# One-token attention plus feed-forward: output in 20 rows of 32, two hardware repeats on TensorE, and the last V in two loads

## The chip, the cores and the metric

The kernel runs on one NeuronCore of one Trainium2 chip. The metric is the device time of one execution in microseconds (us). Every number below comes from result lists, from the profile of one execution of a kernel, or from the packet and instruction records in its trace. The span in a profile is about 2 us shorter than the device time of the same execution (1285.6 against 1287.6 us for the kernel before). In the views, PE is TensorE, PEld its loading of weights, DVE is VectorE, ACT is ScalarE, and SPq and DVEq are instructions that SyncE and VectorE handle without computing (the issue of a load, a wait). A hardware repeat is a loop whose body stands in the program once (in the trace of the changed kernel each turn of the new repeats leaves a counter step of 0.032 to 0.042 us and a branch on TensorE, 0.207 to 0.231 us where it was taken); PV is the product of the softmax weights with V.

## The reference

A decode step: one token `x` of 640 numbers is layer-normalised, then goes through attention over a cache of 32 heads with 32,768 positions, and beside it through a small gated feed-forward part; both results are added to `x`.

```python
x = A_x                                    # (1, 1, 640) bf16
xn = _layernorm(x)
q = (xn @ wq).reshape(B, Sq, 32, 128)      # 32 heads of 128
scores = einsum("bhqd,bhkd->bhqk", q, k_cache) * 128 ** -0.5
o = einsum("bhqk,bhkd->bhqd", softmax(scores), v_cache)
return x + o.reshape(...) @ wo + (silu(xn @ w_gate) * (xn @ w_up)) @ w_down
# k_cache, v_cache: (1, 32, 32768, 128) bf16: 8 MiB per head and cache
```

Each cache byte is used once. 64 loads of 8 MiB make 537 of the 554 MB that the kernel reads.

## The kernel before

SyncE issues all large loads, in one order, into a ring of three slots. A slot is loaded again when its user is done: K when the scores of its head are made, V when its PV product is made.

```python
TAIL = [128, 64, 32, 32]                  # the last V in four loads
WTAIL = [8, 8, 8, 5, 2, 1]                # the output weights in six
...
elif u[0] == "k":
    e.dma_start(ring[:, s, :], kv_src(A_k_cache, u[1], 0, NJ)).then_inc(s_slot[s], 16)
    owner[s] = (s_qk, NHF * (u[1] + 1))   # this slot is free after these scores
elif u == LASTV:
    for i, n in enumerate(TAIL): ...      # one load and one semaphore for each piece
elif u[0] == "v":
    e.dma_start(ring[:, s, :], kv_src(A_v_cache, u[1], 0, NJ)).then_inc(s_slot[s], 16)
    owner[s] = (s_pv, u[1] + 1)           # free after this PV
```

TensorE's program is written out for q and for the first two heads, then a hardware loop runs ten times over three heads, and then the tail is written out. The parts that the change touches:

```python
for b in range(NQB):                      # q: 8 x 5 matmuls of 512 columns
    for c in range(NCD):
        mm = t.matmul(bank[b], lhsT=xnb[:, c, :], rhs=wq_v[:, c, b * 512:(b + 1) * 512], ...)
...
for j in range(first, first + PARTS[part], W):       # PV of one head: 64 matmuls of 512 columns
    mm = t.matmul(O, lhsT=P[:, h % PR, j:j + W], rhs=ring[:, s, j * DH:(j + W) * DH], ...)
...
# the end: acc (128 x 5) holds feed-forward and attention, summed in PSUM
v.tensor_tensor(out=outb[:, :], in0=xr[:, :], in1=acc, op=ALU.add)           # + x, VectorE
t.matmul(orow_ps, lhsT=outb[:, :], rhs=ident[:, :], start=True, stop=True)    # turn to 5 rows of 128
v.tensor_copy(out=orow[:, :], in_=orow_ps)                                    # to bf16 in SBUF
e.dma_start(out[0, 0:1, :].rearrange("o (c m) -> (o c) m", c=NCD), orow[:, :])
```

Of the kernel before, what the change touches and what calls it, by code (L numbers as in the profile page):

```python
# [5 lines left out]
ALU = mybir.AluOpType  # L6
ACTF = mybir.ActivationFunctionType
AX = mybir.AxisListType
BF16 = mybir.dt.bfloat16
F32 = mybir.dt.float32  # L10


def bass_parallel_sum__gqa_block_cached__swiglu_ffn__decode_kernel(
# [13 lines left out]
    H = A_k_cache.shape[1]  # L27
    SK = A_k_cache.shape[2]
    DH = A_k_cache.shape[3]
    F = B_w_gate.shape[1]  # L30
    assert DH == 128 and A_wq.shape[1] == H * DH and D % 128 == 0 and SK % 128 == 0
    NCD = D // 128
    NJ = SK // 128
# [4 lines left out]
    CE = NJ * DH  # L38
# [3 lines left out]
    NQB = (H * DH) // 512  # L42
    SLOTS = 3
    H0, PER = 2, 3
    PR = 3
    SR = 3
    TAIL = [128, 64, 32, 32]
    RB = DH // 32
    OC = H * DH // 128
    WTAIL = [8, 8, 8, 5, 2, 1]  # L50
    PARTS = [64, 64, 128]
# [27 lines left out]
    with ExitStack() as es:  # L79
        def sbt(name, shape, dtype):  # L80
            return es.enter_context(nc.sbuf_tensor(name, shape, dtype))
# [16 lines left out]
        ot = sbt("ot", [128, OC], BF16)  # L98
        hcol = sbt("hcol", [128, FB + 1], BF16)
        par = sbt("par", [128, 2], F32)  # L100
        sg = sbt("sg", [128, 2, FB], F32)
        one1 = sbt("one1", [1, 1], BF16)
        xf = sbt("xf", [128, NCD], F32)
        xr = sbt("xr", [128, NCD], F32)
        orow = sbt("orow", [NCD, 128], BF16)
        xc = sbt("xc", [128, NCD], F32)
        xq = sbt("xq", [128, NCD], F32)
        xn = sbt("xn", [128, NCD], BF16)
        outb = sbt("outb", [128, NCD], BF16)
        st = sbt("st", [128, 8], F32)  # L110
        pmax = sbt("pmax", [128, SR], F32)
        m1 = sbt("m1", [1, SR], F32)
# [91 lines left out]
            return tile[:, bass.ds(start, n)]  # L204

        with nc.psum_tensor("ps8", [128, 8, 512], F32) as ps8:
            bank = [ps8[:, b, :] for b in range(8)]
            O = ps8[0:W, 4, :]
            OL = ps8[:, 5, 0:1]
# [1 line left out]
            acc = ps8[:, 6, 0:NCD]  # L211
            fold_ps = ps8[:, 6, 8:9]
            misc = ps8[:, 7, :]
            orow_ps = ps8[0:NCD, 5, 128:256]
            ffn = bank[0]

            @block.sync
            def sp(e):
                owner = {}
                for u in units:  # L220
                    s = slot_of[u]
                    if s in owner:
                        e.wait_ge(*owner.pop(s))
                    if u[0] == "wq":
                        owner[s] = (s_q, NQB)
                    elif u[0] == "k":
                        e.dma_start(ring[:, s, :], kv_src(A_k_cache, u[1], 0, NJ)).then_inc(s_slot[s], 16)
                        owner[s] = (s_qk, NHF * (u[1] + 1))
                    elif u == LASTV:
                        j = 0  # L230
                        for i, n in enumerate(TAIL):
                            e.dma_start(ring[:, s, j * DH:(j + n) * DH],
                                        kv_src(A_v_cache, u[1], j, n)).then_inc(s_tail[i], 16)
                            j += n
                    elif u[0] == "v":
                        e.dma_start(ring[:, s, :], kv_src(A_v_cache, u[1], 0, NJ)).then_inc(s_slot[s], 16)
                        owner[s] = (s_pv, u[1] + 1)
                    elif u[0] == "ffn":
                        e.dma_start(wg, B_w_gate.rearrange("(p c) n -> p (c n)", c=NCD)).then_inc(s_ffn[0], 16)
                        e.dma_start(wu, B_w_up.rearrange("(p c) n -> p (c n)", c=NCD)).then_inc(s_ffn[1], 16)  # L240
                        e.dma_start(flat[:, d0:d0 + FM * D], B_w_down[0:FM * 128, :].rearrange(
                            "(p j) n -> p (j n)", j=FM)).then_inc(s_ffn[2], 16)
                        e.dma_start(wdr, B_w_down[FM * 128:F, :].rearrange(
                            "f (t n) -> (f t) n", t=2)).then_inc(s_ffn[2], 16)
                    else:
                        wo_src = A_wo.rearrange("(p j) n -> p (j n)", j=OC)
                        j = 0
                        for i, n in enumerate(WTAIL):
                            e.dma_start(wo[:, j * D:(j + n) * D], wo_src[:, j * D:(j + n) * D]).then_inc(s_wo[i], 16)  # L249
                            j += n  # L250
                e.wait_ge(s_fin, 2)
                e.dma_start(out[0, 0:1, :].rearrange("o (c m) -> (o c) m", c=NCD), orow[:, :]).then_inc(s_out, 16)

            @block.gpsimd
            def pool(g):
                n = [0]

                def done(ins):
                    ins.then_inc(s_const, 1)
                    n[0] += 1  # L260
                    g.wait_ge(s_const, n[0])

                for t in (ident, identf):
                    done(g.memset(t[:, :], 0.0))
                    done(g.affine_select(out=t[:, :], in_=t[:, :], compare_op=ALU.not_equal, fill=1.0, base=0,
                                         pattern=[[-1, 128]], channel_multiplier=1))
                done(g.memset(blk[:, :], 0.0))
                for a in range(RB):
                    done(g.tensor_copy(out=fold32[a * 32:(a + 1) * 32, :],
                                       in_=ident[a * 32:(a + 1) * 32, a * 32:a * 32 + OC]))  # L270
                for a in range(RB):
                    done(g.memset(blk[a * 32:(a + 1) * 32, a:a + 1], 1.0))
                assert n[0] == 5 + 2 * RB
                g.wait_ge(s_out, 16)

            @block.tensor
            def pe(t):
# [14 lines left out]

                t.wait_ge(s_a, 11)
                t.wait_ge(s_wq, 16)
                for b in range(NQB):
                    for c in range(NCD):
                        mm = t.matmul(bank[b], lhsT=xnb[:, c, :], rhs=wq_v[:, c, b * 512:(b + 1) * 512],  # L297
                                      start=(c == 0), stop=(c == NCD - 1))
                    mm.then_inc(s_q, 1)
                t.wait_ge(s_qc, NQB)  # L300
                t.wait_ge(s_const, 4)

                def again(out, lhsT, rhs, stop):

# [9 lines left out]
                def scores(h):  # L314
                    kv = ring[:, slot_of[("k", h)], :].rearrange("p (j d) -> p j d", d=DH)
                    for i in range(NHF):
# [9 lines left out]
                                mm = again(ob, ident[:, :], src, g == DH // G - 1)  # L326
                        mm.then_inc(s_qk, 1)

                def pv_part(h, part):
                    s = slot_of[("v", h)]  # L330
                    if part == 0:
                        wait(s_exp, h, lambda h: h + 1)
                        wait(s_o4, h, lambda h: h)
                        wait(s_slot[s], h, lambda h: 16 * use_of[("v", h)])
                    first = sum(PARTS[:part])
                    for j in range(first, first + PARTS[part], W):
                        mm = t.matmul(O, lhsT=P[:, h % PR, j:j + W], rhs=ring[:, s, j * DH:(j + W) * DH],  # L337
                                      start=(j == 0), stop=(j + W == NJ))
                    if part == len(PARTS) - 1:
                        mm.then_inc(s_pv, 1)  # L340
# [66 lines left out]
                def down():  # L407
                    t.wait_ge(s_ffn[2], 32)
                    t.wait_ge(s_fd, 6)
                    for j in range(FM):  # L410
                        for c in range(NCD):
                            t.matmul(acc[:, c:c + 1], lhsT=wd_v[:, j, c, :], rhs=hcol[:, j:j + 1],
                                     start=(j == 0 and c == 0), stop=False, skip_group_check=True)
                    for half in range(2):
                        a, b = half * (D // 2), (half + 1) * (D // 2)
                        for c in range(a // 128, (b + 127) // 128):
                            m0, m1 = max(a, c * 128), min(b, c * 128 + 128)
                            t.matmul(acc[m0 - c * 128:m1 - c * 128, c:c + 1], lhsT=wdr[:, m0 - a:m1 - a],
                                     rhs=hcol[:, FM + half:FM + half + 1],
                                     start=False, stop=False, skip_group_check=True)  # L420
# [21 lines left out]
                fold(H - 2)  # L442
                pv_last(range(1, len(TAIL))).then_inc(s_pv, 1)
                hidden_part(0)
                t.wait_ge(s_const, 5 + 2 * RB)
                t.wait_ge(s_ob, 1)
                t.matmul(op, lhsT=oblk[:, :, :], rhs=fold32[:, :], start=True, stop=True).then_inc(s_op, 1)
                hidden_part(1).then_inc(s_f, 1)
# [1 line left out]
                t.wait_ge(s_ot, 1)  # L450
                project().then_inc(s_att, 1)
                t.wait_ge(s_fin, 1)
                t.matmul(orow_ps, lhsT=outb[:, :], rhs=ident[:, :], start=True, stop=True).then_inc(s_or, 1)

            @block.scalar
            def act(a):
# [50 lines left out]
            def dve(v):  # L507
# [78 lines left out]
                def twice(i):  # L586
# [8 lines left out]
                v.wait_ge(s_rz, H)  # L595
                v.tensor_scalar(out=ocol[:, h:h + 1], in0=OL, scalar1=rzb[:, h % SR:h % SR + 1],
                                scalar2=None, op0=ALU.mult).then_inc(s_ov, 1)
                v.wait_ge(s_const, 5 + 2 * RB)
                v.wait_ge(s_ov, H + 1)
                v.tensor_tensor(out=oblk[:, :, :], in0=ocol[:, :, None].to_broadcast([128, H, RB]),  # L600
                                in1=blk[:, None, :].to_broadcast([128, H, RB]), op=ALU.mult).then_inc(s_ob, 1)
# [12 lines left out]
                                op=ALU.mult).then_inc(s_fd, 1)  # L614
                v.tensor_scalar(out=hcol[:, FM:FM + 2], in0=par[:, :], scalar1=sg[:, 0, FM:FB],
                                scalar2=ffn[:, FB + FM:2 * FB], op0=ALU.mult, op1=ALU.mult).then_inc(s_fd, 1)
                v.wait_ge(s_xr, 1)
                v.wait_ge(s_att, 1)
                v.tensor_tensor(out=outb[:, :], in0=xr[:, :], in1=acc, op=ALU.add).then_inc(s_fin, 1)
                v.wait_ge(s_or, 1)  # L620
                v.tensor_copy(out=orow[:, :], in_=orow_ps).then_inc(s_fin, 1)

# [29 lines left out]
```

## Time and profile before

| | value | from |
|---|---|---|
| device time | 1287.33 us (1287.29 to 1287.57, 3 runs) | result |
| loads on queue q1 | 554.00 MB, 99.7% of sixteen DMA engines' span | page, part 3 |
| TensorE, VectorE busy | 81%, 52% | page, part 1 |
| one 8 MiB load after the other | every 19.35 us, first to last head | packet records |

The page of the kernel before, cut to its span, the busy time of TensorE, the DMA rows of the 40 slices (tenths busy, then GB/s) and the DMA queues (packets, MB, share of 16 engines):

```profile
span 1285.6 us, 9851 instructions
...
PE 1042.0 (81%) x5154; PEld 260.9 (20%) x3235; DVE 672.2 (52%) x409; ACT 52.1 (4%) x139; POOL 2.5 (0%) x17
...
DMA  9999999999999999999999999999999999999998
...
q1 hardware_dynamic: 11242, 554.00, 99.7%
q8 instruction: 9, 0.15, 0.0%
```

The DMA row has no slice under 9 until the last. The kernel's length is the time that the sixteen engines need for these bytes, plus 1.03 us before the first packet and 3.07 us after the last weights have landed (packet records). A chain of waits that names K, PE and DVE by turns through the middle of such a kernel is true and of no use: it shows what released each issue, and every issue was early. The timeline of the kernel before shows how early (start, length, engine, line, operation, count):

```profile
15.35 10.43 PE L297 MATMUL ps<-ring 128*128 128x512 bf16 x39 [10.75 <-DMA ring<-in_A_wq_dram]
...
79.41 0.33 SPq L236 DMA_DIRECT2D ring<-in_A_v_cache_dram  x1
...
86.95 7.07 PE L337 MATMUL ps<-ring,P 128*4 128x512 bf16 x32
...
94.05 0.33 SPq L227 DMA_DIRECT2D ring<-in_A_k_cache_dram  x1
```

The issue at 94.05 us loads K3, after the first head's PV. The load before it (V1, issued at 79.41 us) keeps the engines busy until about 112 us (its last completion write is at 112.02 us). The last stretch is another matter. The chain of waits of the kernel before, its last pieces (start, length, what):

```profile
1253.03 28.77 DMA ring<-in_A_wo_dram
...
1281.85 1.49 PE ps L428 x40
...
1283.36 0.02 DVEq L618
...
1283.43 0.17 DVE outb L619
...
1283.65 0.28 PE ps L453
...
1283.95 0.28 DVE orow L621
```

After the fourth piece of the output weights has landed there is nothing to hide behind: projection, a separate wait instruction of VectorE (L618), add of x, turn (a matmul that transposes), cast, then the issue of the output, in the timeline:

```profile
1284.26 0.36 SPq L252 DMA_DIRECT2D out_dram<-orow  x1
```

### The profile page before, as it was taken

Reading aid. Unit: us, or ns where it says so; the run is one execution under the profiler, and the core shown is the slowest. Engines: PE = TensorE matmul, PEld = TensorE weight load, DVE = VectorE, ACT = ScalarE, POOL = GpSimd, SP = SyncE. Lnnn points to the kernel's source line nnn. Section 1 sums busy time; section 2 is a strip of 40 time slices with the busy share of each in tenths; the row PEclk is TensorE's granted clock in tenths of the full one; section 3 lists DMA queues with packets and bytes.
Section 4 is the critical chain, followed back from the end, with each engine's and each line's share of the span. In section 5 each row is a group of like instructions: output and inputs, shape, how many; then the busy total and the mean of one; then the engine's idle time right before and its main releaser. Section 6 shows DMA issues by size and latency. Waiting matters only on the chain.

```text
span 1285.6 us, 9851 instructions
## 1 busy us (share of the span) xinstructions
PE 1042.0 (81%) x5154; PEld 260.9 (20%) x3235; DVE 672.2 (52%) x409; ACT 52.1 (4%) x139; POOL 2.5 (0%) x17
## 2 busy tenths in 40 slices
PE   3599777889787799778788777898777798778797
PEld 1012112221112221112221112221112221112227
DVE  0855665445665446664446664446664446654441
ACT  2000000000000000000000000000000000000000
POOL 0000000000000000000000000000000000000000
PEclk9799888999888898888998888998888998888995
DMA  9999999999999999999999999999999999999998
GB/s 424 425 445 433 427 430 441 428 432 440 432 432 428 440 430 430 442 430 432 428 440 430 430 442 430 432 428 440 430 430 442 430 432 428 440 430 430 442 413 365
DMA packets 11256, 554.17 MB, mean 431 GB/s; under 512 B 1259, under 2 KB 1516, under 8 KB 1772
## 3 DMA queue, kind: packets, MB, share of 16 engines
q1 hardware_dynamic: 11242, 554.00, 99.7%
q8 instruction: 9, 0.15, 0.0%
q14 instruction: 3, 0.02, 0.0%
q10 hardware_dynamic: 2, 0.00, 0.0%
HBM read 553.99 MB, written 0.00 MB: 431 GB/s over the span
## 4 chain that ended last, share of the span: by engine, by line
DMA 53%; PE 28%; DVE 12%; issue 6%; SPq 0%; DVEq 0%
DMA ring<-in_A_k_cache_dram 51%; PE ps L337 17%; DVE ring L554 12%; PE ps L305 9%; DMA ring<-in_A_wo_dram 2%; PE ps L324 1%; PE ps L379 0%; PE ps L373 0%; PE ps L367 0%; PE ps L428 0%; SPq L249 0%; DVEq L554 0%; DVE sc L560 0%; DVE pmax L566 0%; DVE m L569 0%
## 5 line engine op out<-in xcount | busy, mean ns | idle before, releaser
L554 DVE TENSOR_TENSOR ring<-ring,qb 128x8192 bf16<-128x8192 bf16 x128 | 557.8, 4420 | 315.6 <-DMA ring<-in_A_k_cache_dram 315.6
L305 PE MATMUL ps<-ring,ident 128*128 128x512 bf16 x1920 | 498.4, 418 | 0.0
L337 PE MATMUL ps<-ring,P 128*4 128x512 bf16 x1984 | 443.3, 379 | 0.0
L324 PE MATMUL ps<-ring,ident 128*128 128x512 bf16 x128 | 56.1, 439 | 220.1 <-DVE ring L554 219.7
L337 PEld LDWEIGHTS ps<-ring,P 128*4 128x4 bf16 x1984 | 163.4, 85 | 237.8
L324 PEld LDWEIGHTS ps<-ring,ident 128*128 128x128 bf16 x128 | 12.6, 99 | 618.3 <-DVE ring L554 359.5
L560 DVE TENSOR_REDUCE sc<-ps 128x64 f32<-128x512 f32 x128 | 82.2, 683 | 63.4 <-PE ps L305 63.4
L572 DVE TENSOR_SCALAR negb<-ps 128x1 f32<-128x1 f32 x32 | 5.1, 159 | 108.4 <-PE ps L379 108.4
L480 ACT ACTIVATE P<-sc,negb 128x256 bf16<-128x256 f32 x32 | 16.2, 507 | 957.7 <-DVE negb L572 957.7
L569 DVE TENSOR_REDUCE m<-ps 1x1 f32<-1x128 f32 x32 | 8.9, 279 | 85.2 <-PE ps L373 85.2
L359 PEld LDWEIGHTS ps<-identf,o 4*128 4x128 f32 x248 | 30.7, 190 | 13.1 <-issue 13.1
L359 PE MATMUL ps<-identf,o 4*128 4x1 f32 x248 | 33.3, 251 | 0.0
L367 PEld LDWEIGHTS ps<-rsum,ones 128*128 128x128 f32 x64 | 12.1, 190 | 99.7 <-issue 98.9
L471 ACT ACTIVATE o<-ps,rzb 4x512 f32<-4x512 f32 x31 | 21.0, 678 | 6.2 <-PE ps L337 6.2
L297 PE MATMUL ps<-ring 128*128 128x512 bf16 x39 | 10.4, 428 | 10.8 <-DMA ring<-in_A_wq_dram 10.7
L476 ACT ACTIVATE ocol<-ps 128x1 f32 (+1 forms) x31 | 5.4, 173 | 222.4 <-PE ps L359 222.4
L566 DVE TENSOR_REDUCE pmax<-sc 128x1 f32<-128x256 f32 x32 | 13.4, 420 | 0.0
L373 PE MATMUL ps<-identf,pmax 128*1 128x128 f32 x64 | 12.2, 273 | 1.2 <-DVE pmax L566 1.2
L379 PE MATMUL ps<-m,ones 1*128 1x1 f32 x64 | 12.1, 256 | 0.4 <-DVE m L569 0.4
L379 PEld LDWEIGHTS ps<-m,ones 1*128 1x128 f32 x64 | 9.4, 182 | 14.2 <-issue 13.5
L403 PE MATMUL ps<-xn,ring 128*128 128x1 bf16 x140 | 8.3, 196 | 1.3 <-issue 1.3
L542 DVE RECIPROCAL rzb<-ps 128x1 f32<-128x1 f32 x32 | 5.0, 157 | 8.1 <-PE ps L367 8.1
(66 smaller groups left out, 82.5 us busy)
## 6 DMA issues: line engine op xcount, KB each, us to landing
ring<-in_A_wq_dram SPq DMA_DIRECT2D x1, 5120.0 KB, 15.2
ring<-in_A_v_cache_dram SPq DMA_DIRECT2D x1, 4096.0 KB, 31.8
ring<-in_A_wo_dram SPq DMA_DIRECT2D x3, 1280.0 KB, 24.7
ring<-in_B_w_gate_dram SPq DMA_DIRECT2D x1, 2160.0 KB, 23.2
ring<-in_B_w_up_dram SPq DMA_DIRECT2D x1, 2160.0 KB, 27.9
ring<-in_B_w_down_dram SPq DMA_DIRECT2D x1, 2080.0 KB, 31.3
ring<-in_A_v_cache_dram SPq DMA_DIRECT2D x1, 2048.0 KB, 36.4
ring<-in_A_v_cache_dram SPq DMA_DIRECT2D x2, 1024.0 KB, 39.4
```

Source lines behind the costliest of these rows:

```text
L305: return t.add_instruction(mybir.InstMatmult(start_tensor_calc=False, stop_tensor_calc=stop, tile_size=(128, 128), tile_position=(0, 0), l ...
L324: t.matmul(ob, lhsT=ident[:, :], rhs=src, start=True, stop=False)
L337: mm = t.matmul(O, lhsT=P[:, h % PR, j:j + W], rhs=ring[:, s, j * DH:(j + W) * DH], start=(j == 0), stop=(j + W == NJ))
L359: mm = t.matmul(fold_ps, lhsT=o4[:, m * DH:(m + 1) * DH], rhs=identf[0:W, m:m + 1], start=(m == 0), stop=(m == W - 1))
L367: t.matmul(misc[:, 129:130], lhsT=ones[:, :], rhs=rsum[:, h % SR:h % SR + 1], start=True, stop=True).then_inc(s_z, 1)
L373: t.matmul(misc[0:1, 0:128], lhsT=pmax[:, h % SR:h % SR + 1], rhs=identf[:, :], start=True, stop=True).then_inc(s_t, 1)
L379: t.matmul(misc[:, 128:129], lhsT=ones[0:1, :], rhs=m1[0:1, h % SR:h % SR + 1], start=True, stop=True).then_inc(s_b, 1)
L471: a.activation(out=o4[:, :], in_=O, func=ACTF.Copy, scale=rzb[0:W, h % SR:h % SR + 1]).then_inc(s_o4, 1)
L480: a.activation(out=P[:, h % PR, :], in_=sc[:, :], func=ACTF.Exp, bias=negb[:, h % SR:h % SR + 1], scale=c_scale, accum_out=rsum[:, h % SR: ...
L554: v.tensor_tensor(out=kh, in0=kh, in1=q[:, None, :].to_broadcast([128, HF, DH]), op=ALU.mult).then_inc(s_mul, 1)
L560: v.tensor_reduce(out=sc[:, i * HF:(i + 1) * HF], in_=bank[i].rearrange("p (j e) -> p j e", e=G), axis=AX.X, op=ALU.add).then_inc(s_red, 1)
L566: v.tensor_reduce(out=pmax[:, h % SR:h % SR + 1], in_=sc[:, :], axis=AX.X, op=ALU.max).then_inc(s_max, 1)
```

## The change

It has three parts. The output's end is made shorter: x enters the sum by a matmul before the projection, so VectorE only copies the sum, and copies it into four columns under a mask, so that one matmul with a folded identity turns it into 20 rows of 32 instead of 5 of 128. The q matmuls and the PV of the heads outside the main loop (in fact the first head) become hardware repeats, which makes TensorE's program shorter. And the last V comes in two loads instead of four.

```diff
-    TAIL = [128, 64, 32, 32]
+    TAIL = [128, 128]
+    RUN = 4
...
-                for b in range(NQB):
+                with t.Fori(0, NQB) as b:
                     for c in range(NCD):
-                        mm = t.matmul(bank[b], lhsT=xnb[:, c, :], rhs=wq_v[:, c, b * 512:(b + 1) * 512],
+                        mm = t.matmul(banks[:, bass.ds(b * 512, 512)], lhsT=xnb[:, c, :],
+                                      rhs=wq[:, bass.ds(b * 512 + c * H * DH, 512)],
...
+                def columns(h, s, first, n):
+                    if first == 0:
+                        t.matmul(O[:, 0:1], lhsT=zero[:, :], rhs=zero[:, 0:1], start=True, ...)
+                    with t.Fori(0, n // (RUN * W)) as b:
+                        for r in range(RUN):
+                            j = first + r * W
+                            t.matmul(O, lhsT=P[:, h % PR, bass.ds(b * (RUN * W) + j, W)],
+                                     rhs=flat[:, bass.ds(b * (RUN * W * DH) + (s * CE + j * DH), W * DH)], ...)
+                    return t.matmul(O[:, 0:1], lhsT=zero[:, :], rhs=zero[:, 0:1], start=False, ...)
...
-                    for j in range(first, first + PARTS[part], W):
+                    if group[0] is None:                  # outside the main loop: the first head
+                        mm = columns(h, s, first, PARTS[part])
+                    for j in range(first, first + (PARTS[part] if group[0] is not None else 0), W):
...
+                    t.matmul(acc, lhsT=ident[:, :], rhs=xr[:, :], start=True, stop=False, ...)   # x, before the rest
...
-                t.matmul(orow_ps, lhsT=outb[:, :], rhs=ident[:, :], start=True, stop=True).then_inc(s_or, 1)
+                t.matmul(orow_ps, lhsT=outb[:, :, :], rhs=fold32[:, :], start=True, stop=True).then_inc(s_or, 1)
...
-                v.tensor_tensor(out=outb[:, :], in0=xr[:, :], in1=acc, op=ALU.add).then_inc(s_fin, 1)
+                v.tensor_tensor(out=outb[:, :, :], in0=acc[:, :, None].to_broadcast([128, NCD, RB]),
+                                in1=blk[:, None, :].to_broadcast([128, NCD, RB]), op=ALU.mult).then_inc(s_fin, 1)
```

## The prediction

> **What bounds the kernel now.** The loads. On the page, queue q1 takes 99.7% of sixteen DMA engines' span and moves 554.00 MB at 431 GB/s (PE 81%, DVE 52% busy). The trace's packet records show every engine moving 65,536-byte packets back to back, 2.42 us each, and each whole K or V load of a head ends 19.35 us after the one before, from 14 us to 1234 us, without a gap. So nothing that PE, DVE or ACT does before about 1250 us matters unless it delays the issue of a load past the end of the queued ones. The timeline puts the slack at 10 to 20 us (K3 is issued at 94.05 us, while V1's data run until about 112 us).
>
> **What the change does, part by part.**
>
> 1. *Repeats on PE* (40 q matmuls become 8 turns of 5; the first head's 64 PV matmuls become 4, 4 and 8 turns of 4, plus 4 zero matmuls). Q took 10.4 us and head 0's PV 14.6 us. [...] under loads already queued: worth 0. What it does remove is instruction bytes, about 135 PE instructions. [...] q8 shows 9 packets of 16,384 bytes, four by 198 us, five from 1256.8 to 1281.8 us. Each holds one DMA engine about 1.0 us and makes its next packet 0.47 us slower, about 1.5 us on one engine. The ninth should go; the others come 137 instructions later. But [...] only the slowest counts: at the end the engines finish between 1280.2 and 1282.5 us, and the ninth fetch (1281.8 us) disturbed no packet of the last one. Worth 0 to 0.2 us.
>
> 2. *Last V in two loads.* Its four pieces took 19.58 us (1234.67 to 1254.25 us) where a whole V takes 19.35; the half piece took 9.72. Two halves should take 19.44: 0.14 us, on the critical path as everything queues behind.
>
> 3. *Output.* After the last weights land, the chain is: projection matmuls to 1283.34, DVE add 0.17, turn 0.28, cast 0.28, issue 0.36 us, landing near 1285.1 us. The add becomes a masked multiply of 128x20 (estimate 0.19). The turn streams 32 columns instead of 128 (the other 32-column matmul takes 0.19), the cast is 20x32 instead of 5x128 (estimate 0.18, from small DVE operations at 0.16). Net minus 0.15 to 0.2 us. 20 rows of 64 bytes should land like 5 of 256. The matmul that adds x lies off the path.
>
> Sum: minus 0.4 us. **Predicted 1286.9 us, 1286.2 to 1287.8.** Chances: faster by over 2% 0.005, within 2% 0.99, slower by over 2% 0.005.
>
> **What would show it.** Right: q1 still 99.7%; K and V still 19.35 us apart; q8 with 8 packets and none after about 1281 us; V's last part landing 0.1 to 0.15 us sooner; the DVE cast 0.16 to 0.2 us and the turn about 0.19 us; K3 issued later, with no gap in the DMA row. Wrong: a hole in the DMA row near 50 to 130 us; a cast or output landing not shorter; a last fetch on the slowest engine.
>
> **What would make it wrong.** A repeat so slow (over 10 us) that queued loads run out; a fetch shifted onto an engine already late, up to 1.5 us slower; 64-byte writes landing later; another start-up spread.

The sum came to minus 0.4 us, from 0 for the loop work, 0 to 0.2 us for fewer fetches, 0.14 us for the last V and 0.15 to 0.2 us for the output. Without a measurement behind it: that the ninth fetch should go, and so the 0 to 0.2 us, was my estimate, as no trace had yet shown how many instructions one fetch brings; the 0.19 us of the multiply was an estimate beside the add's 0.17 us; and that 20 rows land like 5 was assumed (measured below: 0.035 us later).

## The result, and the profile after

The changed kernel took 1287.11 us (median of 4 runs, 1286.92 to 1287.31), the kernel before 1287.45 us (4 runs with those above, 1287.29 to 1287.61). The ratio is 0.9997, with a 95% interval of 0.998 to 1.0015: the same at 2%. A ratio here is the mean time of one kernel's fast runs over that of the other's of the same rounds, so not quite the ratio of the medians. By itself this is too little to call a gain. Over all calls the kernel before ran 31 times (mean 1287.34 us, standard deviation 0.14) and the changed kernel 9 times (mean 1287.02 us, 0.17), so a gain of about 0.3 us is there; each of the two calls that ran both kernels shows it (0.34 and 0.48 us).

The page of the changed kernel:

```profile
span 1285.3 us, 10032 instructions
...
DMA  9999999999999999999999999999999999999998
...
q1 hardware_dynamic: 10974, 554.00, 99.7%
q8 instruction: 9, 0.15, 0.0%
```

The same bytes and the same share, in 268 fewer packets (two loads fewer are 2 x 144, the output's further rows and completions add 20). The instruction packets are still nine. The timeline of the changed kernel at the same places:

```profile
15.91 10.57 PE L301 MATMUL ps<-ring 128*128 x40 [11.17 <-DMA ring<-in_A_wq_dram]
...
79.73 0.33 SPq L239 DMA_DIRECT2D ring<-in_A_v_cache_dram  x1
...
87.32 7.13 PE L342 MATMUL ps<-ring,P 128*4 x32
...
94.48 0.33 SPq L230 DMA_DIRECT2D ring<-in_A_k_cache_dram  x1
```

The repeats cost almost nothing: q 10.57 us against 10.43, the second half of the first PV 7.13 against 7.07. From V1's issue to K3's it is 14.75 us against 14.64. And the end of the chain of waits of the changed kernel:

```profile
1252.98 28.71 DMA ring<-in_A_wo_dram
...
1281.73 1.47 PE ps L451 x40
...
1283.22 0.19 DVE outb L641
...
1283.46 0.22 PE ps L476
...
1283.70 0.18 DVE orow L644
```

The issue of the output, in the timeline:

```profile
1283.90 0.39 SPq L255 DMA_DIRECT2D out_dram<-orow  x1
```

The turn went from 0.28 to 0.22 us and the cast from 0.28 to 0.18, while the masked multiply costs 0.02 us more than the add. Two more steps changed. The add had two waits before it and the multiply has one; the separate wait instruction (DVEq L618) is gone from the chain, and VectorE starts 0.20 us after the start of the last projection matmul instead of 0.27. And from the issue to the last written row it now takes 0.90 us instead of 0.86.

To see the loads themselves, I take the completion writes from the packet records. In the packet records of both kernels each load ends with writes of 4 bytes and 9 ns (median): 16 for each load of 128 partitions, 5 for the old output of 5 rows, 10 for the new one of 20 rows (1253 writes in the kernel before, 1226 in the changed one). I read them as one from each engine that takes part. By these writes (from the trace's packet records, us):

```
                                   before            changed
last K, slowest engine             1234.666          1234.637
last V, slowest engine             1254.249 (+19.58) 1254.067 (+19.43)
last weights, slowest engine       1282.496          1282.358
last output row                    1285.111 (+2.62)  1284.789 (+2.43)
```

This is the whole difference: 0.15 us in the last V, 0.19 us in the output, and a small remainder. I take the spread of the sixteen engines for the noise. Right at the first load the slowest engine ends 1.10 us after the fastest in one profile and 1.39 us in the other; by the last K it is 1.77 and 1.79 us, after four instruction fetches of which each set one engine back (see the dose of instructions). A second profile of the changed kernel has its last weights at 1281.99 us instead of 1282.36.

### The profile page after: what moved, and what is told of

Read it like the earlier page. It is cut to its first block, busy times and chain, and to the rows that moved or that the text cites. A ratio compares the mean times of both kernels' runs of the same rounds, so it can differ in the third digit from the quotient of the medians.

```text
span 1285.3 us, 10032 instructions
## 1 busy us (share of the span) xinstructions
PE 1041.2 (81%) x5160; PEld 261.3 (20%) x3240; DVE 672.3 (52%) x409; ACT 52.1 (4%) x139; POOL 2.6 (0%) x18
## 3 DMA queue, kind: packets, MB, share of 16 engines
q1 hardware_dynamic: 10974, 554.00, 99.7%
## 4 chain that ended last, share of the span: by engine, by line
DMA 53%; PE 28%; DVE 12%; issue 6%; DVEq 0%; SPq 0%
DMA ring<-in_A_k_cache_dram 51%; PE ps L358 16%; DVE ring L577 12%; PE ps L310 9%; DMA ring<-in_A_wo_dram 2%; PE ps L342 1%; PE ps L329 1%; PE ps L400 0%; PE ps L394 0%; PE ps L388 0%; PE ps L451 0%; SPq L252 0%; DVEq L577 0%; DVE sc L583 0%; DVE pmax L589 0%
## 5 line engine op out<-in xcount | busy, mean ns | idle before, releaser
L358 PE MATMUL ps<-ring,P 128*4 128x512 bf16 x1920 | 429.0, 379 | 0.0
L358 PEld LDWEIGHTS ps<-ring,P 128*4 128x4 bf16 x1920 | 158.1, 85 | 230.1
L301 PE MATMUL ps<-ring 128*128 x40 | 10.6, 432 | 11.2 <-DMA ring<-in_A_wq_dram 11.2
L342 PE MATMUL ps<-ring,P 128*4 x64 | 14.4, 379 | 0.0
```

Of the source, the lines that this page charges most:

```text
L342: t.matmul(O, lhsT=P[:, h % PR, bass.ds(b * (RUN * W) + j, W)], rhs=flat[:, bass.ds(b * (RUN * W * DH) + (s * CE + j * DH), W * DH)], star ...
```

## The experiments

My theory (A): the loads bound the kernel up to the last weights. So the gain is the last V's saved pieces, plus the shorter end; the repeats give nothing. The rivals: all of the gain is in one part; or fewer instruction bytes are what helps; or TensorE's early work is on the critical path after all. Times are medians of 4 or 5 runs, beside the kernel before of the same rounds.

### Each part alone

The kernel before with only the last V in two loads:

```diff
-    TAIL = [128, 64, 32, 32]
+    TAIL = [128, 128]
```

> The kernel before, with only the last V cut into two loads instead of four. Theory A (the loads bound it and each extra piece costs engine time): the last V's final piece lands about 19.44 us after the last K instead of 19.58 us, and the whole is about 0.14 us shorter than the kernel before, with the output chain unchanged (turn 0.28, cast 0.28 us). Rival B (the whole 0.34 us gain is the shorter output chain): no change from the kernel before. Timing noise is about 0.15 us, so the landings in the trace decide.

The kernel before with only the new output (all lines of the diff that touch `xr`, `outb`, `orow` and their matmuls):

> The kernel before, with only the new output: x added by a matmul, masked multiply, turn to 20 rows of 32. Theory A: turn 0.28 to 0.20 us, cast 0.28 to 0.18 us, so the output load's issue follows the last weights 0.17 to 0.25 us sooner and the time falls by about 0.2 us; the last V still takes 19.58 us. From issue to the last written row stays at 0.85 us[...]. Rival B: all of the 0.34 us is here.

The kernel before with only the repeats (the lines with `Fori`, `columns` and `zero`):

> The kernel before, with only q and the first head's PV as hardware repeats. Theory A (off the critical path): 0.0 us, within 0.2 us either way through the engine on which the instruction packets fall; still 9 instruction packets of 16 KiB, later by about 137 instructions; K3 issued within 0.5 us of before. Rival C (fewer instruction bytes are what saves time): 0.1 to 0.3 us faster.

```
                before   this      difference   last K to last V   last weights to last output row
V alone         1287.34  1287.11   -0.23        19.43              2.61
output alone    1287.34  1287.17   -0.17        19.58              2.43
repeats alone   1287.34  1287.39   +0.05        19.58              2.56
(all three)     1287.45  1287.11   -0.34        19.43              2.43
```

The times alone would not carry a verdict, as each difference is hardly more than the runs' scatter. The two right columns do: they move only in the run that has the part in question, by 0.15 us and by about 0.2 us. No single part holds the whole gain, and the repeats hold none. The output row also settles how 20 rows of 64 bytes land: from issue to last row they took 0.894 to 0.899 us in the ten profiles with the new output, and 5 rows of 256 took 0.859 to 0.864 us in the four with the old one. So they do not land alike, as had been expected, but 0.035 us later.

The whole kernel was run once more as a yardstick for later runs:

> The changed kernel once more, as the yardstick for the other runs of this call. 0.2 to 0.4 us faster than the kernel before of the same rounds if the first result holds.

It took 1286.88 us against 1287.36, 0.48 us faster; last K to last V and last weights to last output row are then 19.43 and 2.36 us.

### A dose of pieces

The changed kernel with the last V in sixteen loads:

```diff
-    TAIL = [128, 128]
+    TAIL = [16] * 16
```

> The changed kernel, with the last V cut into sixteen loads instead of two, a dose of the disputed cost. Theory A: three more pieces cost 0.23 us against a whole V, so 0.077 us for each; fourteen more make the last V about 1.07 us longer (20.5 us instead of 19.43), and the whole kernel 0.9 to 1.3 us slower than the changed one. Rival B: pieces cost nothing on the way, under 0.2 us.

The DMA view of this run (operation, count, KB each, us to landing):

```profile
ring<-in_A_v_cache_dram SPq DMA_DIRECT2D x16, 512.0 KB, 24.5
```

1287.93 us, 0.82 us over the changed kernel's 1287.11 of another call and 0.59 us over the kernel before of the same rounds. By the packet records the last V took 20.45 us, as expected. With the one-load run below (19.35 us) this makes a line: 1, 2, 4 and 16 pieces took 19.35, 19.43, 19.58 and 20.45 us, or 0.073 to 0.077 us for each further piece. The time fell 0.1 us short of the range by the changed kernel's first call; by its second (1286.88 us) it would be 1.05 us and inside, so I don't explain that 0.1 us. The rival that pieces are free is out.

The packets show what a piece costs. A load of 128 partitions has 144 packets, one for each partition and sixteen completion writes of 9 ns; that is eight data packets for each of sixteen engines (8 times 2.42 us is the 19.35 us of a whole load). A packet of 65,536 bytes took 2422 ns (median), one of 32,768 took 1217 and one of 4,096 took 162, where a half and a sixteenth of the first would be 1211 and 151. So each further packet costs 6 to 11 ns, and eight of them with one completion 0.06 to 0.09 us: the price of a piece is mostly that of its packets. A fixed price for each load is not told apart from it, as every run here cut V into loads of 128 partitions.

### A dose of delay on TensorE

Multiplications of V by zero were added to the first head's PV. They add zeros, so the result stays right.

```diff
                         mm = columns(h, s, first, PARTS[part])
+                        if part == 0:
+                            with t.Fori(0, 110) as b:       # and 24 in a second run
+                                t.matmul(O, lhsT=zero[:, :], rhs=ring[:, s, 0:W * DH], start=False, ...)
```

> The changed kernel, with 110 matmuls by zero added in the first head's PV, about 24 us, a dose of delay on PE where the repeats were added. Theory A (PE has about 16 us of slack there, since the queued loads run until 112 us and K3 is issued at 94.5 us): K3 is issued near 118.5 us, the DMA row shows a hole of 6 to 9 us near 112 to 120 us, and the whole is 6 to 9 us slower, not 24 and not 0. Rival F (PE's work there is on the critical path): 24 us slower. Rival G (the loads catch up later): no change.

It took 1314.93 us against 1287.25, 27.7 us slower. At first sight this is the rival's result (24 us and all of it passed on). The profile says otherwise, because the dose was larger than planned. The timeline of this run:

```profile
83.02 40.37 PE L359 MATMUL ps<-ring,zero 128*4 128x512 bf16 x110
...
136.84 0.33 SPq L230 DMA_DIRECT2D ring<-in_A_k_cache_dram  x1
```

110 matmuls took 40.37 us, 0.367 us for each turn of the repeat with one matmul in it, where such matmuls follow one another every 0.22 us without a repeat (32 in 7.07 us in the kernel before). In the trace's instruction records each turn of this repeat has a counter step of 0.036 us and a compare-and-branch of 0.208 us on TensorE (0.207 to 0.213 us where it was taken, 0.076 us where it left the repeat). There is no address work, as this repeat's matmul has fixed addresses; in the PV repeats of the changed kernel, where the addresses move, each such instruction takes 0.074 us (median). Of the 0.244 us of counter and branch 0.15 us of a turn shows (0.367 less 0.22); the rest is hidden behind the matmul. So K3 was issued at 136.84 us instead of 94.48, 42.4 us later. Of these, 27.7 us came through and 14.7 us did not. The windows view of the same run, columns as the first line names them, shows the loads running dry (the last two columns are DMA share and GB/s):

```profile
core 0: us, PE busy (x) PEld busy (x) DVE busy (x) ACT busy (x) POOL busy (x), PEclk, DMA share, GB/s
100.00:110.00 10.00, 9.73 (x27) 2.08 (x26) 0.00 (x0) 0.00 (x0) 0.00 (x0) 1.00 0.97 419
110.00:120.00 10.00, 9.75 (x27) 2.08 (x26) 0.00 (x0) 0.00 (x0) 0.00 (x0) 1.00 0.00 0
120.00:130.00 10.00, 9.65 (x38) 2.97 (x37) 1.81 (x3) 0.60 (x2) 0.00 (x0) 1.00 0.00 0
130.00:140.00 10.00, 9.50 (x41) 2.10 (x26) 10.00 (x3) 0.68 (x1) 0.00 (x0) 1.00 0.30 105
140.00:150.00 10.00, 10.00 (x48) 0.29 (x3) 7.95 (x5) 0.00 (x0) 0.00 (x0) 1.00 0.97 419
```

The engines work at 419 GB/s until the queued loads end near 111 us, and then stand still. What is lost there did not come back: the loads ran at 419 GB/s after the gap as before it, and the run ended 27.7 us later. The rival of catching up is out as well. The smaller dose:

> The changed kernel with 24 matmuls by zero added in the first head's PV, a small dose. In the larger dose one turn of such a repeat took 0.367 us, so about 8.8 us here. Theory A (slack): in the larger dose the first head's PV ended 42.4 us later and the kernel 27.7 us later, so 14.7 us were absorbed; 8.8 us are under that: K3 is issued near 103.3 us, the loads show no hole, and the time is the changed kernel's within 0.2 us. Rival F (a delay there passes on in part at any size): several us slower.

K3 was issued at 103.61 us:

```profile
103.61 0.33 SPq L230 DMA_DIRECT2D ring<-in_A_k_cache_dram  x1
```

That is 9.1 us later than in the changed kernel, and the time was 1286.94 us beside the changed kernel's 1286.88 in the same rounds. The same windows view shows no dip:

```profile
100.00:110.00 10.00, 9.71 (x45) 1.24 (x15) 10.00 (x3) 0.68 (x1) 0.00 (x0) 1.00 0.97 419
110.00:120.00 10.00, 10.00 (x49) 1.51 (x16) 5.92 (x7) 0.00 (x0) 0.00 (x0) 1.00 0.97 420
```

So a delay of 9 us there costs nothing, one of 42 us costs 28, and the 0.1 us that the repeats add lies far within the slack.

### A dose of instructions

The kernel before, with 26 heads written out ahead of the loop instead of 2:

```diff
-    H0, PER = 2, 3
+    H0, PER = 26, 3
```

> The kernel before, with 26 heads written out ahead of the loop instead of 2: the same work, about 5,500 more PE instructions. A dose of instruction fetches. Theory A (each 16 KiB fetch holds one of the sixteen DMA engines for about 1.5 us, and the slowest engine sets the end): about 30 instruction packets instead of 9; 21 more over 16 engines add 31 us of engine time, 2.0 us on average and 1.5 to 3 us on the slowest, so 1.5 to 3 us slower. Rival E (fetches ride along for nothing): no change, within 0.3 us.

1291.77 us against 1287.25: 4.5 us slower, more than I had expected. Its page:

```profile
span 1289.8 us, 9555 instructions
...
q1 hardware_dynamic: 11242, 554.00, 99.5%
q8 instruction: 31, 0.51, 0.2%
```

Fewer instructions run than before (loop bookkeeping is gone), the same bytes are loaded, and 22 more instruction packets are fetched. That about 30 packets would come was my estimate, as no run before this one had shown how many instructions one packet brings. Here it is about 250, again an estimate: a turn of three looped heads has 713 instruction records on TensorE in the kernel before, so 24 written-out heads are about 5,500 without the loop's bookkeeping, for 22 more packets. In the packet records each fetch of 16 KiB holds its engine for about 1.0 us, where a packet of 16 KiB of data takes 0.62 us (the last V's second load in the kernel before), and that engine's next 64 KiB packet takes 2.88 to 2.97 instead of 2.42 us: about 1.5 us for one fetch. Shared evenly, 22 of them would be 2.0 us for each engine. They are not shared evenly: at the last K the slowest engine was 6.2 us behind the fastest (1.77 us in the kernel before), and it landed at 1239.06 us instead of 1234.67, 4.4 us or three fetches later. That fetches are free is out.

The completion writes also tell on which engines the fetches fall. Where q8 fetches, one of the sixteen completion times falls back by 1.5 us against the even pace of 19.35 us for a load, and it is the same one that the fetch eight before had set back. One engine was 1.68 us behind after the second fetch (105.9 us), 3.21 after the tenth (443.5 us), 4.72 after the 18th (793.4 us) and 6.23 after the 26th (1133.5 us). So the fetches of queue q8 went round eight of the sixteen engines in turn. By the last K there had been 26 of them: two engines had taken four, six had taken three, and eight none; six of these eight were still within 0.4 us of the pace. (Of the other two, one was 1.19 us late from the first K on, and one was set back by about 0.95 us by each of three packets of queue q14, which I take for VectorE's, as its program grew too: 6 packets instead of 3.) In the kernel before, only four q8 fetches had come by the last K, at most one on an engine. Three more on the slowest are 4.5 us, and it was 4.4 us later. The expectation had the price of a fetch right and its sharing out wrong.

### Can it be made better?

The changed kernel with the last V in one load and the output weights in five:

```diff
-    TAIL = [128, 128]
+    TAIL = [256]
-    WTAIL = [8, 8, 8, 5, 2, 1]
+    WTAIL = [16, 8, 5, 2, 1]
...
-                pv_last([0])
                 fold(H - 2)
-                pv_last(range(1, len(TAIL))).then_inc(s_pv, 1)
+                pv_last([0]).then_inc(s_pv, 1)
```

So TensorE's order changed as well: all products of the last V now come after the fold of the head before.

> The changed kernel with the last V in one load instead of two, and the output weights in five loads instead of six (the first two joined). Theory A (each piece costs engine time, 0.07 to 0.08 us): V takes 19.35 us instead of 19.43, and the whole is 0.12 to 0.16 us faster than the changed kernel, so near 1286.97 us, as PE still has time to spare (it waits 1.8 us for each of the first two pieces of the output weights). Rival D (the early pieces are needed so that PE starts sooner): 0.3 us or more slower.

1287.15 us against 1287.25: not the 1286.97 expected. The last V did take 19.35 us. But from the last weights to the last output row it was 2.71 us instead of 2.4, and the timeline shows a pause in the last projection for which there is no wait on data (it is not shown whether the joined weights or the new order put it there):

```profile
1281.19 1.02 PE L451 MATMUL ps<-ot,ring 128*128 128x1 bf16 x27 [0.72 <-DMA ring<-in_A_wo_dram]
1282.54 0.49 PE L451 MATMUL ps<-ot,ring 128*128 128x1 bf16 x13 [0.33 <-issue]
```

The changed kernel with every looped head's PV as repeats, too (the condition on the main loop taken out, and with it the written-out PV):

```diff
-                    if group[0] is None:
+                    if True:
                         mm = columns(h, s, first, PARTS[part])
```

> The changed kernel with the PV of every head but the last as hardware repeats, not only the first head's. About 230 fewer PE instructions in the program, so one instruction packet fewer before the last load lands (8 instead of 9 in all, or the ninth after the end). Theory A: PE's loop work hides under the loads, K and V still 19.35 us apart; time within 0.3 us of the changed kernel, perhaps 0.1 us faster. Rival H (three nested repeats per head and four zero matmuls slow each head): loads spaced more than 19.35 us apart, and the time clearly longer.

1286.82 us against 1287.25, 0.43 us faster than the kernel before, which is what the changed kernel itself shows (0.34 and 0.48 us). K and V came 19.35 us apart as ever, and its instruction packets are eight. With the output weights in five loads on top:

> PV of all heads but the last as repeats, and the output weights in five loads instead of six. One piece fewer is worth 0.05 to 0.08 us of engine time, and there is no PE pause for instructions inside the last projection, as the last instruction packet there came at 1282.2 us without the fifth-piece change. Expected 1286.75 us, 0.1 us under the all-repeats run. Rival: the joined first piece holds PE up at the end and gives it back.

1287.80 us against 1287.36, slower, and with a wider scatter (1287.21 to 1288.51). The rival's time came out; its reason is not shown. From the last weights to the last output row it took 3.18 us, where the all-repeats run took 2.35. The timeline:

```profile
1281.52 0.35 PE L451 MATMUL ps<-ot,ring 128*128 128x1 bf16 x7 [0.72 <-DMA ring<-in_A_wo_dram]
1282.74 1.02 PE L451 MATMUL ps<-ot,ring 128*128 128x1 bf16 x33 [0.87 <-issue]
1283.80 0.18 DVE L641 TENSOR_TENSOR outb<-ps,blk 128x20 bf16<-128x20 f32 x1 [10.31 <-PE ps L451]
```

TensorE stops after 7 of the last 40 matmuls. The last instruction packet before that ended 1.5 us ahead of the moment when it goes on. The same holds for every such pause inside a stretch of one-column matmuls: there are sixteen of them, of 0.2 to 2.2 us, in eleven of the thirteen profiles with an unlooped tail, and each time TensorE went on 1.3 to 1.6 us after the end of an instruction packet. Most hide. The kernel before has one of 1.34 us in its feed-forward matmuls which the changed kernel, with its instructions in other places, doesn't have; its last projection then starts at 1273.7 instead of 1275.0 us and waits for the same weights. So I read them as TensorE having run out of instructions; no run took the fetch alone away. In the all-repeats run with six pieces that packet began at 1278.8 us, with five pieces at 1280.1 us. TensorE's first 40 projection matmuls had then to wait for the joined piece. That the small early piece lets TensorE reach its fetch point sooner is argued from these two times, not shown, and so is that the pause is a fetch at all.

Last, the tail's 256 one-column matmuls as repeats of 16 to save instructions:

```diff
...
-                        for _ in range(TAIL[i]):
-                            mm = t.matmul(OL, lhsT=ring[:, s, j * DH:(j + 1) * DH], rhs=P[:, h % PR, j:j + 1], ...)
+                        with t.Fori(0, TAIL[i] // 16) as b:
+                            for r in range(16):
+                                t.matmul(OL, lhsT=flat[:, bass.ds(b * (16 * DH) + (s * CE + (j + r) * DH), DH)],
+                                         rhs=P[:, h % PR, bass.ds(b * 16 + j + r, 1)], ...)
...
```

> The same as the run with all PV as repeats and five output-weight loads, with the last head's 256 one-column matmuls as repeats of 16 too. About 470 fewer PE instructions, so two instruction packets fewer in the tail (6 in all), and no PE pause for instructions in that stretch (0.4 to 2.2 us in the others). Theory A (fetches on the slowest engine matter): 0 to 0.3 us faster. Rival I (address work in the repeat makes each 27 ns matmul several times longer, so the tail's PE work runs late): PE's last V stretch longer than 20 us instead of 8 to 10 us, and the whole 1 us or more slower.

1321.38 us, 34 us slower. The timeline, one turn to a line:

```profile
1283.71 2.53 PE L374 MATMUL ps<-P,ring 128*128 x16 [0.45 <-issue]
1286.73 2.48 PE L374 MATMUL ps<-P,ring 128*128 x16 [0.49 <-issue]
```

A turn of sixteen takes 2.5 us and 0.45 us more to the next, 0.186 us for a matmul that takes 0.027 us when it is written out, as the timeline of the kernel before shows:

```profile
1252.83 3.46 PE L349 MATMUL ps<-P,ring 128*128 128x1 bf16 x128
```

Within a turn the matmuls start 0.153 us apart, and before each stands an instruction that works out its addresses, 0.074 us long in the trace's instruction records (FUSED_REGOPS). The last V's products end at 1301 us, 39 us later than in the changed kernel, with all weights long there. Only six instruction packets are fetched, and it helps nothing.

No version clearly beats the changed kernel.

## Why the prediction was right or wrong

Predicted were 1286.9 us with a range of 1286.2 to 1287.8, and "within 2%" with 0.99; measured were 1287.11 us, and 1286.88 us in a second call.

- *The loads bound it: right.* q1 stayed at 99.7%, and the loads stayed 19.35 us apart. The two doses of delay confirm the slack: predicted 10 to 20 us, measured 14.7 us.
- *Repeats worth 0: right*, alone +0.05 us. The loop work was overestimated; the figure had no measurement behind it. 0.1 us was measured from V1's issue to K3's.
- *The ninth fetch should go: wrong,* and my estimate only. There are nine in both profiles; the last only moved from 1281.8 to 1282.9 us, after the last weights, where no load was left for it to delay. Why taking out about 135 instructions did not drop it, no run shows.
- *How the fetches are shared among the engines: wrong.* The forecast's clause on this rested on no trace; the expectation of the dose had them nearly evenly shared. In the run with 31 fetches, the 26 before the last K went round eight of the sixteen engines, and the slowest was late by three fetches more, where an even share of the 22 further ones is a little over one.
- *Last V, 0.14 us: right.* 19.58 to 19.43 us, and 0.073 to 0.077 us for a piece at 1, 2, 4 and 16 pieces.
- *Output, 0.15 to 0.2 us: right in the sum, in part by luck.* From the last weights to the last output row it took 2.54 to 2.62 us in the four profiles with the old output and 2.35 to 2.43 us in those with the new one in which TensorE's last projection was neither paused nor late. The steps that the prediction named gave 0.15 us: multiply 0.02 more, turn 0.07 less (0.09 forecast), cast 0.10 less. Two that it lacked gave another 0.035 us together: VectorE started 0.07 us sooner, with one wait instruction fewer, and the 20 rows landed 0.035 us later, where they were to land like 5.
- *The sum of 0.4 us* was measured as 0.34 and 0.48 us. The intervals in the trace show 0.15 + 0.19 us; what the sum counted for fewer fetches (0 to 0.2 us) is not in them. I take the rest for noise, the spread of the engines, which the prediction named last.

## What to carry to other kernels

Where the DMA row is full from end to end, cost a change only by what it does to the engines' work (bytes; packets, here 0.073 to 0.077 us for a further piece of V; instruction fetches, here about 1.5 us on one engine) and to the stretch after the last byte; measure the slack of all else with a dose of delay, and check the size of the dose in the trace. A hardware repeat hid behind matmuls of 512 columns with four in a turn (7.13 against 7.07 us), showed with one in a turn (0.367 against 0.22 us), and cost several times the work with one-column matmuls (0.186 against 0.027 us). When the expected gain is smaller than the scatter of the runs, read the two or three intervals in the trace that the change should move: here they were steady to 0.1 us or better where the total was not.
